# Linear attention with a feed-forward block on one core: softmax reciprocals of k moved to ScalarE, layernorm applies of the k loop moved to VectorE, the Gelu table loaded ahead

## The chip, the cores and the metric

The kernel runs on one core of a Trainium2 chip. The metric is the device time of one execution in microseconds (us), lower being better. One execution of each kernel was profiled. In the profile, PE is TensorE, PEld its weight loads, DVE VectorE, ACT ScalarE and POOL GpSimd; L298 is a line of that kernel's own file, so the same statement has another number in another kernel. All timed runs named here were of the fast state, and comparisons are among those; the one exception, a single look whose state is unknown, is marked.

## The reference, cut to what matters

```python
x = A_x                                            # 1 x 2048 x 640
h = x + A(layernorm(x))                            # linear attention, 32 heads of 20
h2 = h + B(layernorm(h))                           # (gelu(y @ w_gate) * (y @ w_up)) @ w_down

# in A, for each head: q, k, v from x @ wqkv
pq, pk = q @ w_phi, k @ w_phi
phi_q = concat(softmax(pq), softmax(-pq))          # over the 20 features of a head
phi_k = concat(softmax(pk), softmax(-pk))
kv = phi_k^T @ v;  z = sum of phi_k over the sequence
o = (phi_q @ kv) / (phi_q @ z + 1e-6)
```

The sequence is worked in 16 tiles of 128 rows. The softmax of k is not divided out: the kernel keeps E = exp(+-pk), sums it per head (`sk`), and scales v by the reciprocal of the sum (`rs`) instead, once for +pk and once for -pk. So there are two products of v with `rs` per tile, 128x672 elements each.

## The kernel before

The parts that the change touches. `todo` matters: VectorE's product of tile t-1 is put off, and issued between the sum and the reciprocal of tile t.

```python
    def k_tile(t):                       # TensorE: pk; ScalarE: E = exp(+-pk)
        ...
    def k_norm(t):
        sk = small(p1, [P, 2 * H], "sk")
        nc.vector.reduce_sum(sk, Ek[t].rearrange("p s (h f) -> p (s h) f", f=Dh), axis=AX.X)
        if t - 1 in todo:
            todo.pop(t - 1)()
        rs = small(p1, [P, 2 * H], "rs")
        nc.vector.reciprocal(rs, sk)
        Vt[t] = vt = ev.tile([P, 2, H, VC], BF16, name="vt", bufs=8)

        def mult(s, eng):
            eng.tensor_tensor(vt[:, s], vS[t % 6], rs[:, s * H:(s + 1) * H, None].to_broadcast([P, H, VC]), ALU.mult)

        mult(1, nc.gpsimd)
        if t in VP:                      # VP = (0, 2, 4, 6, 9, 11): both products on GpSimd
            mult(0, nc.gpsimd)
        elif t == NT - 1:
            mult(0, nc.vector)
        else:
            todo[t] = lambda: mult(0, nc.vector)
    ...
    for t in range(NT):                  # the k loop, NT = 16
        k_tile(t)
        if t in FQ:                      # FQ = (4, 5, 6, 7, 8): one block of Wq2 a tile,
            fold(WqT, Wq2, True, ...)    # its cast on ScalarE or VectorE by turns
        for j in range(len(QT)):         # QT = (15, 15, 15, 15): after tile 15 the first
            if t == QT[j]:               # four groups of q and their Exp
                q_mm(j)
                q_exp(j)
        if t + 4 < NT:
            v_tile(t + 4)                # TensorE: pv; ScalarE: vS
        if t > 0 and t + 6 < NT:
            ln_ap(t + 6, on_act=True)    # layernorm apply on ScalarE, transposed by DMA
        if t % 2 == 0 and t + 8 < NT:
            ln_st(t + 8, t + 9)          # VectorE: statistics
        k_norm(t)
        if t % 2 == 1 and t >= 5:
            kv_tile(t - 5)               # TensorE: kvp += E^T @ vt
            kv_tile(t - 4)
    ...
    for t in range(12, NT):
        kv_tile(t)
    kv_mask()
    ...                                  # groups q+4.. of q, attention of tiles 0 and 1
    weave(gus(0, 0, 256) + downs(0, (0, 1)), ... attn_at(3, 1, SHORT) ...)
    weave(gus(0, 256, 512) + downs(0, (2, 3)), attn_at(7, 1, SHORT2))
    for b in range(1, NB): ...           # blocks 1 to 3
```

Three words of it: `fold` multiplies one 128-row block of the q weights by w_phi on TensorE (tile `wa`), and a cast on ScalarE or VectorE brings it to `Wq`. `weave` issues a list of TensorE groups, called units here (`gus` are gate and up, `downs` the down projection), and `attn_at(tile, unit, offsets)` says at which unit each of the eight attention stages of a tile goes in between.

The softmax here doesn't subtract the row's maximum and nothing guards it: scores larger than these inputs give would overflow.

Of the kernel before, what the change touches and what calls it, by code (L numbers as in the profile page):

```python
# [8 lines left out]
BF16 = mybir.dt.bfloat16  # L9
F32 = mybir.dt.float32  # L10
ALU = mybir.AluOpType
ACTF = mybir.ActivationFunctionType
AX = mybir.AxisListType
# [4 lines left out]
def kernel(  # L18
# [12 lines left out]
    nc = tc.nc  # L31
    P = 128
    S = 2048
    D = 640
    H = 32
    Dh = 20
    FF = 1536
    NT = S // P
# [9 lines left out]
    VP = (0, 2, 4, 6, 9, 11)  # L48
# [6 lines left out]
    VC = Dh + 1  # L55
# [30 lines left out]
    nhalf = const.tile([P, 2], F32, name="nhalf")  # L86
# [6 lines left out]
    def small(pool, shape, name, bufs=3):  # L93
        return pool.tile(shape, F32, name=name, bufs=bufs)

    def gtile(name):
        return psG.tile([P, 2, 512], F32, name=name, tag="G")

    def ln_stats(pool, tiles, tag, act=True, between=None):

        n = len(tiles)
        mv = small(pool, [P, n, nc.vector.BN_AGGR_DIM], "mv" + tag)
        stats = small(pool, [P, n, 2, nc.vector.BN_STATS_DIM], "stats" + tag)
        for j, xt in enumerate(tiles):
            for i in range(2):
                nc.vector.bn_stats(stats[:, j, i, :], xt[:, i * HD:(i + 1) * HD])  # L106
                if between and i == j == 0:
                    between()
        for j in range(n):
            nc.vector.bn_aggr(mv[:, j, :], stats[:, j])  # L110
        ve = small(pool, [P, n], "ve" + tag)
        nc.gpsimd.tensor_scalar_add(ve, mv[:, :, 1], EPS)
        rstd = small(pool, [P, n], "rstd" + tag)
        nc.gpsimd.tensor_tensor(rstd, ve, nhalf[:, 0:n], op=ALU.pow)  # L114

        mr = small(pool, [P, n], "mr" + tag)
        if act:
            for j in range(n):
                nc.gpsimd.tensor_scalar(mr[:, j:j + 1], mv[:, j, 0:1], rstd[:, j:j + 1], -1.0,
                                        op0=ALU.mult, op1=ALU.mult)  # L120
        return [(xt, mv[:, j, 0:1], rstd[:, j:j + 1], mr[:, j:j + 1]) for j, xt in enumerate(tiles)]
# [26 lines left out]
    p1 = p1_cm.__enter__()  # L148
# [1 line left out]
    Wk2 = p1.tile([P, NC, D], BF16, name="Wk2")  # L150
    acc = p1.tile([P, NC, 4, VC], F32, name="acc")

    vS = [p1.tile([P, H, VC], BF16, name=f"vS{i}") for i in range(6)]
    fp_cm = tc.tile_pool(name="fp", bufs=1, side="right", reuse_waits="tile")
    fp = fp_cm.__enter__()
    WkT = fp.tile([P, NC, D], BF16, name="WkT")
# [7 lines left out]
    for c0, c1 in ((0, 2), (2, 4), (4, 5)):  # L164
        nc.sync.dma_start(Wv[:, c0:c1, :], w_v[:, c0:c1, 2 * D:3 * D])

    ones = fp.tile([P, 2], F32, name="ones")
    nc.scalar.activation(ones, nhalf, ACTF.Exp)
    nc.scalar.dma_start(wphi, phi_v.rearrange("(c p) f -> p c f", p=P))
    nc.sync.dma_start(x_sb[1][:, 0:2, :], x_v[:, 4:6, :])  # L170
    nc.scalar.dma_start(x_sb[1][:, 2:4, :], x_v[:, 6:8, :])
# [8 lines left out]

    zero = fp.tile([P, 512], BF16, name="zero")
    nc.vector.memset(zero, 0.0)
    for i in range(6):
        nc.vector.memset(vS[i][:, :, Dh], 1.0)
    make_identity(nc, ident)
    nc.gpsimd.memset(hmask, 1.0)
# [41 lines left out]
    lnp, Ek, Vt = {}, {}, {}  # L228

    def ln_st(*tiles, act=True, between=None):  # L230
        for t, v in zip(tiles, ln_stats(p1, [x_sb[t // 4][:, t % 4, :] for t in tiles], "1", act, between)):
            lnp[t] = v

    def ln_ap(t, on_act=False, on_pe=False):
        ln = (ln_act if on_act else ln_dve)(p1, "1", *lnp[t])
        if on_pe:
            lnp[t] = ln
        else:
            transpose_to(LN1T[t // 4][:, :, t % 4 * P:(t % 4 + 1) * P], ln, False)
# [28 lines left out]
                                 start=(c == 0), stop=(c == NC - 1))  # L268

    def v_ev(t):  # L270
        nc.scalar.copy(vS[t % 6][:, :, 0:Dh].rearrange("p (u h) f -> p u h f", u=2),
                       pv[t][:, :, 0:HD].rearrange("p u (h f) -> p u h f", f=Dh))

    def v_tile(t):
        v_mm(t)
        v_ev(t)

    def k_tile(t):
        pk = gtile("pk")
        proj(pk, t, Wk2)  # L280
        Ek[t] = ev.tile([P, 2, D], BF16, name="E", bufs=8)
        for s in range(2):
            nc.scalar.activation(Ek[t][:, s, :].rearrange("p (u f) -> p u f", u=2), pk[:, :, 0:HD],  # L283
                                 ACTF.Exp, scale=(1.0 if s == 0 else -1.0))

    def k_norm(t):


        sk = small(p1, [P, 2 * H], "sk")
        nc.vector.reduce_sum(sk, Ek[t].rearrange("p s (h f) -> p (s h) f", f=Dh), axis=AX.X)  # L290
        if t - 1 in todo:
            todo.pop(t - 1)()
        rs = small(p1, [P, 2 * H], "rs")
        nc.vector.reciprocal(rs, sk)  # L294
        Vt[t] = vt = ev.tile([P, 2, H, VC], BF16, name="vt", bufs=8)

        def mult(s, eng):
            eng.tensor_tensor(vt[:, s], vS[t % 6], rs[:, s * H:(s + 1) * H, None].to_broadcast([P, H, VC]), ALU.mult)  # L298

        mult(1, nc.gpsimd)  # L300
        if t in VP:
            mult(0, nc.gpsimd)
        elif t == NT - 1:
            mult(0, nc.vector)
        else:
            todo[t] = lambda: mult(0, nc.vector)

    todo = {}

    def kv_tile(t):  # L310

# [29 lines left out]
    def q_exp(j, signs=(0, 1)):  # L341
        for s in signs:
            nc.scalar.activation(Eq[j][:, :, s, :], pqs[j][:, 0:len(QG[j])], ACTF.Exp, scale=(1.0, -1.0)[s])  # L343
# [21 lines left out]
    v_ev(1)  # L365
    v_tile(2)
    ln_st(4, 5, act=False)
    ln_st(6)
    v_mm(3, (0,))
    fold(WkT, Wk2, False, (0, 1))  # L370
    ln_ap(4, on_pe=True)
# [2 lines left out]
    ln_ap(5, on_pe=True)  # L374
    fold(WkT, Wk2, False, (2, 3, 4))
    ln_tp(4, True)
    ln_st(7)
    fp_cm.__exit__(None, None, None)
    ev_cm = tc.tile_pool(name="ev", bufs=1, side="right", reuse_waits="tile")
    ev = ev_cm.__enter__()  # L380
# [1 line left out]
    for t in range(NT):  # L382
        if t == T3:
            ps_cm.close()
            psG = ps_cm.enter_context(tc.tile_pool(name="psG", bufs=3, space=PSUM, reuse_waits="tile"))
            psK = ps_cm.enter_context(tc.tile_pool(name="psK", bufs=1, space=PSUM, reuse_waits="tile"))
            kvp = psK.tile([P, 2, 512], F32, name="kvp")
        k_tile(t)
        if t == 0:
            ln_tp(5)  # L390
            ln_ap(6)
        if t in FQ:
            fold(WqT, Wq2, True, [i for i, f in enumerate(FQ) if f == t])
        for j in range(len(QT)):
            if t == QT[j]:
                q_mm(j)
                q_exp(j)
        if t + 4 < NT:
            v_tile(t + 4)
        if t > 0 and t + 6 < NT:  # L400
            ln_ap(t + 6, on_act=True)
        if t % 2 == 0 and t + 8 < NT:
            ln_st(t + 8, t + 9)
        k_norm(t)
        if t % 2 == 1 and t >= 5:
            kv_tile(t - 5)
            kv_tile(t - 4)
        if t == 9:
            nc.gpsimd.memset(KV, 0.0)
            nc.gpsimd.memset(kmask, 1.0)  # L410
            for r in HALF:
                nc.gpsimd.affine_select(out=kmask[r], in_=kmask[r], pattern=[[4, NC], [-Dh, 4]],
                                        compare_op=ALU.is_ge, fill=0.0, base=0, channel_multiplier=1)
                nc.gpsimd.affine_select(out=kmask[r], in_=kmask[r], pattern=[[-4, NC], [Dh, 4]],
                                        compare_op=ALU.is_ge, fill=0.0, base=Dh - 1, channel_multiplier=-1)
            nc.gpsimd.tensor_copy(KV[:, :, 0, :, KC - 1], kmask)
            nc.gpsimd.tensor_copy(KV[:, :, 1, :, 0], kmask)
        if t == 10:
            nc.sync.dma_start(Wg, wg_v)
            nc.sync.dma_start(Wo, wo_v)  # L420
            nc.sync.dma_start(Wu, wu_v)
# [10 lines left out]
    p2 = ctx.enter_context(tc.tile_pool(name="p2", bufs=1, reuse_waits="tile"))  # L432
# [107 lines left out]
    def attn_ln(t, on_pe=False):  # L540
        st[t] = (ln_dve if on_pe else ln_act)(p2, "2", *st[t])
# [49 lines left out]
    def weave(units, stages):  # L591

        stages = sorted(later + stages, key=lambda x: x[0])
        later.clear()
        for i, (fn, *args) in enumerate(units):
            while stages and stages[0][0] <= i:
                _, g, *a = stages.pop(0)
                g(*a)
            store(1)
            fn(*args)  # L600
        later.extend((i - len(units), g, *a) for i, g, *a in stages)

    def gus(b, a0, a1):
        return [(gate_up, b, f, a0, a1) for f in range(NF)]

    def downs(b, tls):
        return [(down, b, tl, u) for tl in tls for u in range(2)]
# [30 lines left out]
    attn_e(0, True, True)  # L638
    q_mm(q + 6)
    q_exp(q + 6)  # L640
    attn_ln(1, True)
    attn_e(1, True, True)
    attn_a(2, 2)
# [2 lines left out]
    def attn_at(t, i, offs):  # L646

        fns = (attn_a, attn_b, attn_b2, attn_b3, attn_c, attn_d, attn_d2, attn_e)
        return [(i + o, fn, t) for fn, o in zip(fns, offs) if o >= 0]

    SHORT = (0, 2, 3, 4, 9, 9, 10, 12)
    SHORT2 = (0, 2, 3, 4, 10, 10, 11, 13)
# [3 lines left out]
    weave(gus(0, 0, 256) + downs(0, (0, 1)),  # L656
          attn_at(2, 0, (-1, 0, 1, 2, 7, 7, 8, 10)) + attn_at(3, 1, SHORT) + attn_at(4, 6, SHORT2) + attn_at(5, 9, SHORT2) +
          attn_at(6, 13, SHORT2))
    weave(gus(0, 256, 512) + downs(0, (2, 3)), attn_at(7, 1, SHORT2))
    for b in range(1, NB):  # L660
        stages = []
        if b + 1 < NB:
# [34 lines left out]
```

## Time and profile before

| | before |
|---|---|
| time, median of the runs beside the changed kernel | 281.83 us (281.5 to 282.31) |
| span of the profiled execution | 279.4 us |
| TensorE starts pk of tile 0 | 16.86 us |
| starts the first group of q: end of the k loop | 62.36 us |
| starts the fifth group of q: end of the loop's tail | 72.42 us |
| starts the third gate group: Gelu under way | 95.77 us |
| starts the gate groups of block 1 | 144.07 us |

The marks are start times of TensorE matmuls in the timeline. Since TensorE hardly waits between them, the distance of two marks is the time of that part of the program: 45.50 us for the loop, 10.06 for its tail, 23.35 from there to the third gate group, 48.30 from there to block 1. I use the same marks for every kernel below.

The profile's groups of instructions, one shape each, say what the parts cost. The columns are line, engine, operation, output and inputs, shapes, count, then busy us and mean ns of one, then the idle time of the engine ahead of them:

```profile
L298 POOL TENSOR_TENSOR vt<-vS,rs 128x672 bf16<-128x672 bf16 x22 | 29.2, 1345 | 9.1 <-DVE rs L294 8.5 <-ACT E L283 0.4
L290 DVE TENSOR_REDUCE sk<-E 128x64 f32<-128x1280 bf16 x16 | 23.3, 1455 | 3.4 <-ACT E L283 3.4
L298 DVE TENSOR_TENSOR vt<-vS,rs 128x672 bf16<-128x672 bf16 x10 | 8.8, 882 | 0.1
L130 DVE TENSOR_SCALAR ln<-x_sb,mv,rstd 128x640 bf16<-128x640 bf16 x9 | 3.9, 443 | 2.4 <-POOL rstd L114 2.4
```

A product costs 1.35 us on GpSimd and 0.88 on VectorE, a layernorm apply on VectorE 0.44. Now see in the timeline of tile 5 (start, duration, engine, operation) when the two engines multiply:

```profile
34.24 0.85 DVE L298 TENSOR_TENSOR vt<-vS,rs 128x672 bf16<-128x672 bf16 x1
...
35.01 0.55 DVE L294 RECIPROCAL rs<-sk 128x64 f32<-128x64 f32 x1
...
35.64 4.03 POOL L298 TENSOR_TENSOR vt<-vS,rs 128x672 bf16<-128x672 bf16 x3 [0.18 <-DVE rs L294]
```

VectorE's product is over before its reciprocal releases GpSimd. The order of the program keeps the two apart in six of VectorE's ten products (0.85 us each) and lets VectorE begin first in the last (0.86, at 69.12); three near the loop's end begin in the last 0.2 to 0.3 us of a product of GpSimd and take 0.93 to 1.01. I did not see what that was worth when I predicted.

### The profile page before, as it was taken

The numbers are of one execution on the slowest core, as the hardware profiler recorded it, in microseconds if no ns is written. First come the engines' busy times: TensorE is split into PE (matmuls) and PEld (weight loads), VectorE is DVE, ScalarE is ACT, GpSimd is POOL, SyncE is SP. The second block draws the span as 40 slices with busy tenths as digits, with TensorE's granted clock in tenths as the row PEclk, the third lists the DMA queues.
The fourth block names the chain that finished last, engine by engine and source line by source line (L and its number), as shares of the span: only waits on it lengthen the run. The fifth ranks groups of instructions, "written<-read, shape, count | busy, mean of one in ns | idle before, by whom it ended". The sixth has DMA issues, their size and how long they took to land.

```text
span 279.4 us, 5750 instructions
## 1 busy us (share of the span) xinstructions
PE 271.9 (97%) x2326; PEld 171.5 (61%) x2326; DVE 166.0 (59%) x289; ACT 139.9 (50%) x226; POOL 96.5 (35%) x211
## 2 busy tenths in 40 slices
PE   5899999999999999999999999999999999999995
PEld 2676677774655788788764555675455567444573
DVE  5899998789396586676324848322667532333222
ACT  2589888758596847355434454413446340222200
POOL 5448986794302216453401243300135230000000
PEclk9999999999999999999999999999999999999999
DMA  7991323694440021322520103221031513000011
GB/s 231 265 260 25 55 49 46 176 396 158 142 145 0 2 45 29 70 50 68 52 70 2 36 20 66 42 77 47 2 47 23 74 23 94 26 1 0 0 49 47
DMA packets 40347, 21.05 MB, mean 75 GB/s; under 512 B 33152, under 2 KB 38400, under 8 KB 40320
## 3 DMA queue, kind: packets, MB, share of 16 engines
q1 hardware_dynamic: 39376, 20.16, 28.8%
q10 hardware_dynamic: 944, 0.52, 0.7%
q8 instruction: 18, 0.29, 0.5%
q14 instruction: 9, 0.07, 0.1%
HBM read 10.18 MB, written 2.62 MB: 46 GB/s over the span
## 4 chain that ended last, share of the span: by engine, by line
PE 89%; DVE 4%; ACT 3%; DMA 1%; POOL 1%; issue 1%; ACTq 0%
PE gu L554 37%; PE pd L569 19%; PE pq L338 8%; PE po L509 8%; PE pk L251 7%; PE pv L251 5%; PE ab L449 2%; PE kvp L316 2%; DVE stats L106 1%; DMA x_sb<-in_A_x_dram 1%; DVE sk L290 1%; ACT E L283 1%; POOL rstd L114 1%; ACT Eq L343 1%; PE wa L215 1%
## 5 line engine op out<-in xcount | busy, mean ns | idle before, releaser
L557 ACT ACTIVATE g<-gu 128x512 bf16<-128x512 f32 (+1 forms) x60 | 30.7, 512 | 76.1 <-PE gu L554 75.1
L560 DVE TENSOR_TENSOR GT<-gu,g 128x512 bf16<-128x512 f32 (+1 forms) x60 | 34.5, 581 | 53.6 <-ACT g L557 53.4
L554 PE MATMUL gu<-LN2T,Wg 128*128 128x512 bf16 (+1 forms) x300 | 61.9, 337 | 0.5 <-DVE GT L560 0.4
L554 PE MATMUL gu<-LN2T,Wu 128*128 128x512 bf16 (+1 forms) x300 | 61.7, 336 | 0.0
L569 PE MATMUL pd<-Wd,GT 128*128 128x320 bf16 x384 | 53.8, 299 | 0.0
L569 PEld LDWEIGHTS <-GT 128*128 128x128 bf16 x384 | 37.4, 98 | 15.7 <-DVE GT L560 0.9
L554 PEld LDWEIGHTS <-Wu 128*128 128x128 bf16 x300 | 29.4, 98 | 22.6
L554 PEld LDWEIGHTS <-Wg 128*128 128x128 bf16 x300 | 28.4, 98 | 21.3 <-issue 0.5
L251 PEld LDWEIGHTS <-LN1T 128*128 128x128 bf16 x300 | 28.5, 98 | 11.6 <-issue 0.7
L298 POOL TENSOR_TENSOR vt<-vS,rs 128x672 bf16<-128x672 bf16 x22 | 29.2, 1345 | 9.1 <-DVE rs L294 8.5
L575 DVE TENSOR_TENSOR y<-pd,x_sb 128x640 bf16<-128x640 f32 (+1 forms) x17 | 13.3, 784 | 30.6 <-PE pd L569 30.6
L457 ACT COPY AB<-ab 128x704 f32<-128x704 f32 x28 | 19.5, 748 | 13.7 <-PE ab L449 13.5
L290 DVE TENSOR_REDUCE sk<-E 128x64 f32<-128x1280 bf16 x16 | 23.3, 1455 | 3.4 <-ACT E L283 3.4
L490 DVE TENSOR_TENSOR tt<-AB,w 128x1280 bf16<-128x1280 f32 x16 | 23.8, 1486 | 2.1 <-POOL w L483 2.0
L251 PE MATMUL pk<-Wk,LN1T 128*128 128x320 bf16 x160 | 24.1, 299 | 0.4 <-ACT E L283 0.3
L509 PE MATMUL po<-Wo,oT 128*128 128x320 bf16 x160 | 24.4, 299 | 0.0
L283 ACT ACTIVATE E<-pk 128x640 bf16<-128x640 f32 x32 | 20.8, 705 | 6.9 <-PE pk L251 6.7
L338 PE MATMUL pq<-LN1T,Wq 128*128 128x512 bf16 x100 | 22.9, 379 | 0.0
L251 PE MATMUL pv<-Wv,LN1T 128*128 128x320 bf16 x140 | 21.3, 299 | 0.0
L343 ACT ACTIVATE Eq<-pq 128x1024 bf16<-128x1024 f32 (+1 forms) x22 | 19.4, 950 | 3.7 <-PE pq L338 3.7
L509 PEld LDWEIGHTS <-oT 128*128 128x128 bf16 x160 | 15.6, 98 | 7.2 <-ACT oT L139 0.2
L125 ACT ACTIVATE ln<-x_sb,v,rstd 128x640 bf16<-128x640 bf16 x14 | 12.9, 919 | 10.5 <-POOL v L537 10.3
(80 smaller groups left out, 258.8 us busy)
## 6 DMA issues: line engine op xcount, KB each, us to landing
out_dram<-y SPq DMA_DIRECT2D x15, 160.0 KB, 1.8
Wg<-in_B_w_gate_dram SPq DMA_DIRECT2D x1, 1920.0 KB, 7.6
Wu<-in_B_w_up_dram SPq DMA_DIRECT2D x1, 1920.0 KB, 15.1
Wd<-in_B_w_down_dram SPq DMA_DIRECT2D x1, 1920.0 KB, 8.0
x_sb<-in_A_x_dram SPq DMA_DIRECT2D x2, 640.0 KB, 4.7
Wo<-in_A_wo_dram SPq DMA_DIRECT2D x1, 800.0 KB, 9.3
x_sb<-in_A_x_dram SPq DMA_DIRECT2D x2, 320.0 KB, 4.8
Wv<-in_A_wqkv_dram SPq DMA_DIRECT2D x2, 320.0 KB, 6.2
```

The costliest lines, as they stand in the source:

```text
L251: nc.tensor.matmul(ps[:, u, 0:HD], lhsT=lnT(t, c), rhs=W[:, c, u * HD:(u + 1) * HD], start=(c == 0), stop=(c == NC - 1))
L283: nc.scalar.activation(Ek[t][:, s, :].rearrange("p (u f) -> p u f", u=2), pk[:, :, 0:HD], ACTF.Exp, scale=(1.0 if s == 0 else -1.0))
L290: nc.vector.reduce_sum(sk, Ek[t].rearrange("p s (h f) -> p (s h) f", f=Dh), axis=AX.X)
L298: eng.tensor_tensor(vt[:, s], vS[t % 6], rs[:, s * H:(s + 1) * H, None].to_broadcast([P, H, VC]), ALU.mult)
L338: nc.tensor.matmul(pqs[j][:, i, :], lhsT=Wq2[:, kc, c * P:(c + 1) * P], rhs=LN1T[b][:, kc, :], start=(kc == 0), stop=(kc == NC - 1))
L343: nc.scalar.activation(Eq[j][:, :, s, :], pqs[j][:, 0:len(QG[j])], ACTF.Exp, scale=(1.0, -1.0)[s])
L490: nc.vector.tensor_tensor(tt.rearrange("p s (h f) -> p s h f", f=Dh), num, w[:, :, :, None].to_broadcast([P, 2, H, Dh]), ALU.mult)
L509: nc.tensor.matmul(po[:, u, 0:HD], lhsT=st[t][:, c, :], rhs=Wo[:, c, u * HD:(u + 1) * HD], start=(c == 0), stop=(c == NC - 1))
L554: nc.tensor.matmul(gu[:, i, 0:n], lhsT=W[:, c, f * P:(f + 1) * P], rhs=LN2T[b][:, c, a0:a1], start=(c == 0), stop=(c == NC - 1))
L557: nc.scalar.activation(g[:, 0:n], gu[:, 0, 0:n], ACTF.Gelu_apprx_tanh)
L560: nc.vector.tensor_tensor(st[b, "g", f][:, a0:a1], gu[:, 1, 0:n], g[:, 0:n], ALU.mult)
L569: nc.tensor.matmul(pd[:, u, 0:HD], lhsT=st[b, "g", f][:, tl * P:(tl + 1) * P], rhs=Wd[:, f, u * HD:(u + 1) * HD], start=(f == 0), stop=(f ...
```

## The change

The intent: take the slow reciprocal (547 ns a tile) off VectorE by computing 1/S as exp(-ln S) on ScalarE, where Ln and Exp can live in one table set; in exchange move the loop's layernorm applies from ScalarE, where one costs 933 ns, to VectorE, where it costs 443; and load the Gelu table ahead of the first Gelu by a dummy. With `rs` no longer made on VectorE, its products are issued plainly, one tile later, after the sum. A seventh `vS` buffer makes room for the delay, and the attention of tile 7 moves two units later in its weave.

```diff
-    vS = [... for i in range(6)]
+    vS = [... for i in range(7)]                       # and every t % 6 becomes t % 7
-    nc.scalar.activation(ones, nhalf, ACTF.Exp)
+    nc.scalar.add_instruction(mybir.InstLoadActFuncSet(..., act_func_set_id=6))
@@ k_tile, after the two Exp of tile t
+        if t > 0:
+            k_rs(t - 1)
+    def k_rs(t):
+        sk = st1[t]
+        nc.scalar.activation(sk, sk, ACTF.Ln)
+        st1[t] = rs = small(p1, [P, 2 * H], "rs")
+        nc.scalar.activation(rs, sk, ACTF.Exp, scale=-1.0)
@@ k_norm
-        nc.vector.reduce_sum(sk, Ek[t]..., axis=AX.X)
-        if t - 1 in todo:
-            todo.pop(t - 1)()
-        nc.vector.reciprocal(rs, sk)
+        for s in range(2):
+            nc.vector.reduce_sum(sk[:, s * H:(s + 1) * H], Ek[t][:, s, :]..., axis=AX.X)
+    def k_vt(t):
+        for s in (1, 0):
+            eng = nc.gpsimd if s == 1 or t in VP else nc.vector
+            eng.tensor_tensor(vt[:, s], vS[t % 7], rs[...].to_broadcast(...), ALU.mult)
@@ the loop
-            ln_ap(t + 6, on_act=True)
+            ln_ap(t + 6)
-            ln_st(t + 8, t + 9)
+            ln_st(t + 8, t + 9, act=False)           # ln_st(6), ln_st(7) ahead of the loop too
         k_norm(t)
+        if t > 0:
+            k_vt(t - 1)
+        if t == NT - 1:
+            k_rs(t)
+            k_vt(t)
@@ after the last Exp of q
+    nc.scalar.activation(dummy, nhalf, ACTF.Gelu_apprx_tanh)
@@ the second weave
-    ... attn_at(7, 1, SHORT2))
+    ... attn_at(7, 3, SHORT2))
```

More of the change, by code (lines that the diff above doesn't have):

```diff
@@ L151 @@
     acc = p1.tile([P, NC, 4, VC], F32, name="acc")
-    vS = [p1.tile([P, H, VC], BF16, name=f"vS{i}") for i in range(6)]
+    vS = [p1.tile([P, H, VC], BF16, name=f"vS{i}") for i in range(7)]
     fp_cm = tc.tile_pool(name="fp", bufs=1, side="right", reuse_waits="tile")
@@ L165 @@
         nc.sync.dma_start(Wv[:, c0:c1, :], w_v[:, c0:c1, 2 * D:3 * D])
-    ones = fp.tile([P, 2], F32, name="ones")
-    nc.scalar.activation(ones, nhalf, ACTF.Exp)
+    nc.scalar.add_instruction(mybir.InstLoadActFuncSet(name=nc.get_next_instruction_name(), act_func_set_id=6))
     nc.scalar.dma_start(wphi, phi_v.rearrange("(c p) f -> p c f", p=P))
@@ L182 @@
     nc.vector.memset(zero, 0.0)
-    for i in range(6):
+    for i in range(7):
         nc.vector.memset(vS[i][:, :, Dh], 1.0)
@@ L270, in v_ev @@
     def v_ev(t):
-        nc.scalar.copy(vS[t % 6][:, :, 0:Dh].rearrange("p (u h) f -> p u h f", u=2),
+        nc.scalar.copy(vS[t % 7][:, :, 0:Dh].rearrange("p (u h) f -> p u h f", u=2),
                        pv[t][:, :, 0:HD].rearrange("p u (h f) -> p u h f", f=Dh))
@@ L284, in k_tile @@
                                  ACTF.Exp, scale=(1.0 if s == 0 else -1.0))
-    def k_norm(t):
-        sk = small(p1, [P, 2 * H], "sk")
-        nc.vector.reduce_sum(sk, Ek[t].rearrange("p s (h f) -> p (s h) f", f=Dh), axis=AX.X)
-        if t - 1 in todo:
-            todo.pop(t - 1)()
-        rs = small(p1, [P, 2 * H], "rs")
-        nc.vector.reciprocal(rs, sk)
-        Vt[t] = vt = ev.tile([P, 2, H, VC], BF16, name="vt", bufs=8)
-        def mult(s, eng):
-            eng.tensor_tensor(vt[:, s], vS[t % 6], rs[:, s * H:(s + 1) * H, None].to_broadcast([P, H, VC]), ALU.mult)
-        mult(1, nc.gpsimd)
-        if t in VP:
-            mult(0, nc.gpsimd)
-        elif t == NT - 1:
-            mult(0, nc.vector)
-        else:
-            todo[t] = lambda: mult(0, nc.vector)
-    todo = {}
+        if t > 0:
[5 more added lines that the diff above has]
+        nc.scalar.activation(rs, sk, ACTF.Exp, scale=-1.0)
+    st1 = {}
+    def k_norm(t):
+        st1[t] = sk = small(p1, [P, 2 * H], "sk")
+        for s in range(2):
+            nc.vector.reduce_sum(sk[:, s * H:(s + 1) * H], Ek[t][:, s, :].rearrange("p (h f) -> p h f", f=Dh), axis=AX.X)
+    def k_vt(t):
+        rs = st1[t]
+        Vt[t] = vt = ev.tile([P, 2, H, VC], BF16, name="vt", bufs=8)
+        for s in (1, 0):
+            eng = nc.gpsimd if s == 1 or t in VP else nc.vector
+            eng.tensor_tensor(vt[:, s], vS[t % 7], rs[:, s * H:(s + 1) * H, None].to_broadcast([P, H, VC]), ALU.mult)
     def kv_tile(t):
@@ L367 @@
     ln_st(4, 5, act=False)
-    ln_st(6)
+    ln_st(6, act=False)
     v_mm(3, (0,))
@@ L376 @@
     ln_tp(4, True)
-    ln_st(7)
+    ln_st(7, act=False)
     fp_cm.__exit__(None, None, None)
@@ L640 @@
     q_exp(q + 6)
+    dummy = small(p2, [P, 2], "dummy", 1)
+    nc.scalar.activation(dummy, nhalf, ACTF.Gelu_apprx_tanh)
     attn_ln(1, True)
@@ L658 @@
           attn_at(6, 13, SHORT2))
-    weave(gus(0, 256, 512) + downs(0, (2, 3)), attn_at(7, 1, SHORT2))
+    weave(gus(0, 256, 512) + downs(0, (2, 3)), attn_at(7, 3, SHORT2))
     for b in range(1, NB):
```

## The prediction

> **What bounds the kernel now.** I read the page's first two parts, then TensorE's waits, the chain in order of time, and the timeline at the four places that the diff touches: the k loop, its end, the first Gelu, the hand-over to block 1.
>
> ```profile
> PE 271.9 (97%) x2326; PEld 171.5 (61%) x2326; DVE 166.0 (59%) x289; ACT 139.9 (50%) x226; POOL 96.5 (35%) x211
> PEclk9999999999999999999999999999999999999999
> ...
> PE gu L554 <- DVE GT L560: 0.4, 1, 0.4
> PE pk L251 <- ACT E L283: 0.3, 1, 0.3
> ```
>
> TensorE is busy for 97% of the span at full clock. A busy TensorE need not be at its peak, so I checked the chain's pieces: ten matmuls of 320 columns take 1.36 us there, ten of 512 take 2.17, in every stage alike, which is 0.42 ns a column throughout. From 16.86 us to 276.5 the chain is such pieces, apart from a stretch near 21 to 31 us (where TensorE is busy beside it) and one near 91.6 to 95.8. So there is next to nothing to take out of the middle: TensorE's waits after the start-up are 0.3 us for a buffer of pk, 0.4 for one of gu, and some tenths between pieces. The 59% of VectorE is an average: by stretches it is busy 14.36 of the 14.74 us from 16.86 on and 13.88 of the next 14.40. In the k loop it is the second bound.
>
> The loop's end, from the timeline:
>
> ```profile
> 69.03 2.92 ACT L343 ACTIVATE Eq<-pq 128x1024 bf16<-128x1024 f32 x4 [0.22 <-PE pq L338]
> 69.12 0.86 DVE L298 TENSOR_TENSOR vt<-vS,rs 128x672 bf16<-128x672 bf16 x1
> 69.19 1.97 POOL L298 TENSOR_TENSOR vt<-vS,rs 128x672 bf16<-128x672 bf16 x1 [1.34 <-DVE rs L294]
> 70.00 2.36 PEld L316 LDWEIGHTS <-E 128*64 128x64 bf16 x120 [0.42 <-issue]
> 70.00 2.49 PE L316 MATMUL kvp<-vt,E 128*64 128x84 bf16 x120
> ```
>
> The scaled v of the last tile, 15, is made at 69.1 to 71.2 us, while ScalarE works on the four Eq pairs until 71.95; TensorE multiplies tiles 10 to 15 from 70.0 and tile 15 comes last, from about 72.1. It just fits.
>
> The first Gelu:
>
> ```profile
> 91.62 1.94 ACT L343 ACTIVATE Eq<-pq 128x1024 bf16<-128x1024 f32 x2 [0.50 <-PE pq L338]
> 93.58 1.28 ACT L557 ACT_TABLE_LOAD   x1
> 94.88 0.38 ACT L557 ACTIVATE g<-gu 128x256 bf16<-128x256 f32 x1
> 95.29 0.42 DVE L560 TENSOR_TENSOR GT<-gu,g 128x256 bf16<-128x256 f32 x1 [1.20 <-ACT g L557]
> 95.77 0.71 PE L554 MATMUL gu<-LN2T,Wg 128*128 128x256 bf16 x5 [0.37 <-DVE GT L560]
> ```
>
> The load already starts 0.02 us after the last Exp ends; it waits for nothing else. The hand-over of tile 7 to block 1:
>
> ```profile
> 136.09 0.81 DVE L523 SCALAR_TENSOR_TENSOR x_sb<-po,x_sb 128x640 bf16<-128x640 f32 x1
> ...
> 139.75 0.92 ACT L125 ACTIVATE ln<-x_sb,v,rstd 128x640 bf16<-128x640 bf16 x1 [1.49 <-POOL v L537]
> ...
> 144.07 1.25 PE L554 MATMUL gu<-LN2T,Wg 128*128 128x512 bf16 x5
> ...
> LN2T<-ln SPq DMA_TRANSPOSE x14, 2.6
> ```
>
> The layernorm ends at 140.67, the transposing DMA lands 2.6 later, 143.3, and the matmul that needs it starts at 144.07: some 0.8 us of slack.
>
> **What the Trainium skill says.** "ScalarE: Activation LUTs", section "Table sets: the hidden batching unit": one set holds ln and exp, so both need one load. The diff loads a set by number, which I take to be that one; the trace before shows one load at the start and one before Gelu, Copy, Identity and Square running in both; I expect two again. Its section "What ACT_TABLE_LOAD costs" gives an ACTIVATE with immediates 186 ns + 0.833 ns an element: 239 ns for 64, an estimate; the trace agrees roughly (128x2 took 203 ns, 128x512 took 597; the load 1283, as the page has it). "Perfetto Trace Analysis", section "Tensor Engine Instruction (MATMUL, LD_WEIGHTS)", says that ScalarE, VectorE and GpSimd are strict FIFO; the trace agrees, everything in program order. "GPSIMD Engine Reference", section "Specifications", names contention for SBUF with VectorE instructions of two SBUF inputs: a product on GpSimd takes 1.32 us, but 1.97 where VectorE's product of 0.86 starts beside it.
>
> **The change part by part.**
>
> 1. Reciprocals. VectorE loses 16 x 547 ns = 8.8 us. ScalarE gets Ln and Exp per tile: 2 x 239 plus a hand-over, about 0.5 us (estimate), 8 us in all. The sum over h is split: VectorE's products of 256 and 512 elements take 416 and 690 ns, so some 142 ns of an instruction are fixed; I pay them once more a tile, +0.13 where the two overlap a little (estimate), 2 us in all.
>
> 2. Layernorm applies, 9 of them. ScalarE loses 9 x 933 = 8.4 us, VectorE gains 9 x 0.44 = 4.0. GpSimd loses the small products of L119. Sums: ScalarE about -0.4, VectorE -8.8+2+4.0 = -2.8, but nearly all of that after tile 9; while the applies run, VectorE changes by -0.46+0.13+0.40 = +0.07 us a tile (from a start to the next: reciprocal 65.82 to 66.28, apply 9.35 to 9.75).
>
> 3. In the loop TensorE runs without a gap, so less work elsewhere gives at most the 0.3 of the pk wait plus about 0.1. Against it: ScalarE now waits for VectorE. Exp of tile t is followed by Ln of tile t-1, which needs the sum of t-1. Before, the sum of tile 4 ended at 34.33 and Exp of tile 5 at 34.74, that of tile 6 at 41.39 and Exp of 7 at 41.74: 0.4 us of slack. Going through tiles 4 to 9 by hand with these durations, ScalarE, now earlier, waits 0.5 us at each such sum, TensorE gains 0.4 at tile 5 and gives it back in the v buffers at tiles 6 to 9. I put the loop at 0 (-0.4 to +0.8). The seventh vS buffer takes away ScalarE's 1.5 us of waits (vS for vt), inside the same account.
>
> 4. The loop's end. In program order Ln and Exp of tile 15 now stand on ScalarE after the four Eq pairs, which follow TensorE and end at 71.95. So its reciprocals come at 71.95+0.5 = 72.45 instead of 69.0. Then the two products start together: VectorE 0.86, to 73.35; GpSimd 1.97, to about 74.45. TensorE ends tile 14 near 72.1 and waits; ten matmuls of tile 15 follow GpSimd's product, 0.22. The stage ends at 74.7 instead of 72.49: **+2.2 us** (+1.5 if GpSimd takes 1.32). What follows (mask, copy, products: 1.77 us before) still lies behind q's ten matmuls of 2.27.
>
> 5. Gelu's load. It was early already. The dummy ACTIVATE after it takes about 0.2 (203 ns for 128x2) ahead of the first real Gelu, whose product releases the gu buffer TensorE waits for: **+0.15**.
>
> 6. attn 7 two units later. Its last stage then has offset 16 in a weave of 16 units and slips to the head of the next, before block 1's first gate matmul, which needs it. Its po moves from ahead of unit 11 to ahead of unit 13, so after po TensorE has three half downs (6.52 us for four, 1.63 each) and one ab (0.50): 5.39 us. The chain after po, from tile 6, whose Square waits for no Gelu: VectorE starts 131.34, Square 132.20, layernorm 134.53 to 135.45, issue, 2.6 to landing: 138.07, that is 6.73, plus 0.06 from po's end, 6.8. TensorE waits 6.8-5.39 = **+1.4**.
>
> Sum: 0+2.2+0.15+1.4 = 3.75; I take 0.25 off because po, Gelu or GpSimd's product may sit a little better than drawn: +3.5, 281.9+3.5 = **285.4 us**.
>
> **The rivals.** (a) The intended gain: ScalarE and VectorE relieved, TensorE faster. For it: ScalarE's waits for vt, the pk wait. Against: all TensorE waits outside the start-up that these could free sum to under 1 us, so at best 281.0. (b) ScalarE takes VectorE's place and the cross wait breaks the loop: if each of some eight tiles lost 0.5 us more, +4, then 289. For: VectorE 97% busy there. Against: the order of VectorE's work stays the same and its time per tile grows by only 0.07. (c) The loop's end costs nothing: if the products of tile 15 were ready by 72.1, the sum falls to about +1.5, 283.4. Against: ScalarE's order. (d) Sets switch at each Ln: 32 loads of 1.28 us, 41 us; I give it 1%, since one set serves both.
>
> **Range and chances.** The additions at 4 and 6 are independent: losing either gives 283 to 284, the loop going badly adds up to 1, a slowed clock after the pause up to 1.5 (the start-up has a pause of 1.7 us without one). The range is **283.2 to 287.3**. Two per cent are 5.6 us: slower by that needs rival (b), **0.07**; faster needs 5.6 us that TensorE doesn't have, **0.01**; same **0.92**.
>
> **What would show it.** Right: a TensorE wait of about 2 us before kvp's last matmuls, put down to vt on GpSimd; a second of about 1.4 before gu of block 1, released by the DMA into LN2T; the gu wait for GT at 0.5 instead of 0.4; ScalarE waiting for sk in the loop; two table loads. If kvp shows no wait, step 4 is wrong; if gu of block 1 doesn't wait for LN2T, step 6 is; if pv waits for vS by several tenths per tile, step 3 was too kind. A span below 281 would mean that TensorE's pieces themselves became shorter, which nothing here foresees.

## The result, and the profile after

The changed kernel takes 289.59 us (median of 4, 288.89 to 291.28) against 281.83 for the kernel before: the ratio is 1.0283, with a 95% interval of 1.0236 to 1.0329. It is slower by over 2%, and the time lies outside the predicted range. Such a ratio is the mean time of one kernel's fast runs over that of the other's fast runs of the same rounds, so it is not quite the ratio of the medians quoted. The slowest of the four, 291.28, had a mean granted clock of 0.988; the other three lie within 0.75 us.

| part | before | after | difference | predicted |
|---|---|---|---|---|
| start, to pk of tile 0 | 16.86 | 17.43 | +0.57 | 0 |
| k loop, to the first group of q | 45.50 | 49.39 | **+3.89** | 0 (-0.4 to +0.8) |
| tail, to the fifth group of q | 10.06 | 12.51 | +2.45 | +2.2 |
| to the third gate group | 23.35 | 23.44 | +0.09 | +0.15 |
| to block 1 | 48.30 | 49.77 | +1.47 | +1.4 |
| the rest of the span (279.4 and 287.9) | 135.3 | 135.4 | 0 | 0 |

The start is nothing of the change's: over the kernels below, which have the same program up to there but for small things, that mark lies anywhere from 16.49 to 17.69. What is left is the loop. TensorE's waits in the changed kernel (what waited, what ended the wait, us in total, times, longest) show by which doors it came in:

```profile
PE pk L250 <- DVE Wq L225: 2.8, 2, 1.8
PE gu L560 <- DMA LN2T<-ln: 1.4, 1, 1.4
PE kvp L317 <- DVE vt L308: 1.3, 1, 1.3
...
PE wa L214 <- ACT Wq L223: 1.1, 1, 1.1
PE kvp L317 <- POOL vt L308: 0.8, 1, 0.8
...
PE gu L560 <- DVE GT L566: 0.5, 1, 0.5
```

The two waits of kvp are the tail (step 4), the one of gu for LN2T is the hand-over (step 6), and gu for GT is 0.5 where it was 0.4 (step 5): all three as foreseen. New are 2.8 us in which pk waits for VectorE's casts of Wq, and 1.1 us in which the fold waits for ScalarE's. Together they are 3.9 us, the size of the loop's loss. ScalarE's cast comes late because ScalarE stood waiting for VectorE's sum just before it (1.64 us, until 33.12). VectorE's casts and sums come late because its own work has grown:

```profile
L308 POOL TENSOR_TENSOR vt<-vS,rs 128x672 bf16<-128x672 bf16 x22 | 32.5, 1500 | 12.9 <-ACT rs L292 12.8
L300 DVE TENSOR_REDUCE sk<-E 128x32 f32<-128x640 bf16 x32 | 24.4, 804 | 2.5 <-ACT E L282 2.4
L308 DVE TENSOR_TENSOR vt<-vS,rs 128x672 bf16<-128x672 bf16 x10 | 14.7, 1468 | 4.5 <-ACT rs L292 4.5
L130 DVE TENSOR_SCALAR ln<-x_sb,mv,rstd 128x640 bf16<-128x640 bf16 x18 | 9.8, 550 | 2.5 <-POOL rstd L114 2.5
```

The same product of the same size takes VectorE 1468 ns where it took 882: 5.9 us more in ten. The nine layernorm applies of the loop cost 9.8-3.9 = 5.9 us, 0.66 each, where 0.44 were put down. The split sums cost 1.1 us more, not 2. So VectorE, which loses 8.8 us of reciprocals, ends up with 5.9+5.9+1.1-8.8 = 4.1 us more over the whole kernel, where the prediction had it 2.8 us lighter. The timeline of the changed kernel shows what lies beside the long ones:

```profile
28.25 4.56 POOL L308 TENSOR_TENSOR vt<-vS,rs 128x672 bf16<-128x672 bf16 x3
28.49 1.79 DVE L308 TENSOR_TENSOR vt<-vS,rs 128x672 bf16<-128x672 bf16 x1
...
30.20 1.43 DVE L130 TENSOR_SCALAR ln<-x_sb,mv,rstd 128x640 bf16<-128x640 bf16 x1
...
36.33 4.55 POOL L308 TENSOR_TENSOR vt<-vS,rs 128x672 bf16<-128x672 bf16 x3
...
36.59 1.77 DVE L308 TENSOR_TENSOR vt<-vS,rs 128x672 bf16<-128x672 bf16 x1
...
38.28 0.81 DVE L225 CAST Wq<-wa 128x640 bf16<-128x640 f32 x1
...
39.14 1.52 PE L250 MATMUL pk<-Wk,LN1T 128*128 128x320 bf16 x10 [1.84 <-DVE Wq L225]
```

`rs` has been ready since 26.48 and 33.67, and GpSimd starts its products as soon as its own small layernorm work is done, at 28.25 and 36.33, while VectorE is still in the sum; VectorE's product and its apply then run beside them and come out 0.9 and 1.0 us too long. Behind the second such product stands the cast, and behind the cast TensorE, idle for 1.84 us. The tail shows the reverse order of starts:

```profile
76.64 0.26 ACT L292 ACTIVATE rs<-sk 128x64 f32<-128x64 f32 x1
76.93 0.86 DVE L308 TENSOR_TENSOR vt<-vS,rs 128x672 bf16<-128x672 bf16 x1 [4.49 <-ACT rs L292]
76.97 1.99 POOL L308 TENSOR_TENSOR vt<-vS,rs 128x672 bf16<-128x672 bf16 x1 [5.58 <-ACT rs L292]
77.84 0.38 PE L317 MATMUL kvp<-vt,E 128*64 128x84 bf16 x10 [1.27 <-DVE vt L308]
79.01 0.38 PE L317 MATMUL kvp<-vt,E 128*64 128x84 bf16 x10 [0.79 <-POOL vt L308]
```

Here VectorE was idle and began 0.04 us ahead; it took its 0.86, and GpSimd paid with 1.99. As predicted, the products of tile 15 come only after Ln and Exp, which stand behind the four Exp pairs of q.

### The profile page after: what moved, and what is told of

Same layout as the page of the kernel before. It is cut to its first block, busy times and chain, and to the rows that moved or that the text cites. A ratio compares the mean times of both kernels' runs of the same rounds, so it can differ in the third digit from the quotient of the medians.

```text
span 287.9 us, 5757 instructions
## 1 busy us (share of the span) xinstructions
PE 274.6 (95%) x2326; PEld 173.1 (60%) x2326; DVE 170.3 (59%) x299; ACT 138.5 (48%) x249; POOL 95.9 (33%) x201
## 4 chain that ended last, share of the span: by engine, by line
PE 83%; DVE 7%; ACT 4%; DMA 2%; issue 2%; POOL 1%; POOLq 0%; ACTq 0%
PE gu L560 36%; PE pd L575 17%; PE po L515 8%; PE pq L339 7%; PE pk L250 5%; PE pv L250 4%; DVE sk L300 2%; PE ab L455 2%; ACT Eq L344 2%; DVE stats L106 2%; PE pv L266 1%; PE kvp L317 1%; DMA x_sb<-in_A_x_dram 1%; PE tp L138 1%; DVE ln L130 1%
## 5 line engine op out<-in xcount | busy, mean ns | idle before, releaser
L308 POOL TENSOR_TENSOR vt<-vS,rs 128x672 bf16<-128x672 bf16 x22 | 32.5, 1500 | 12.9 <-ACT rs L292 12.8
L300 DVE TENSOR_REDUCE sk<-E 128x32 f32<-128x640 bf16 x32 | 24.4, 804 | 2.5 <-ACT E L282 2.4
```

What stands on the lines that cost most here:

```text
L300: nc.vector.reduce_sum(sk[:, s * H:(s + 1) * H], Ek[t][:, s, :].rearrange("p (h f) -> p h f", f=Dh), axis=AX.X)
L308: eng.tensor_tensor(vt[:, s], vS[t % 7], rs[:, s * H:(s + 1) * H, None].to_broadcast([P, H, VC]), ALU.mult)
```

## The experiments

**Theory.** VectorE's products and applies collide with GpSimd's products over access to SBUF. The Trainium skill says this on a page that the prediction did not use: "SBUF — State Buffer", section "Who interferes with whom", lets a VectorE instruction with two SBUF inputs, or one in a 2-port mode (which a tensor_scalar can enter), contend with GpSimd (the former where GpSimd's instruction reads SBUF, as its products do), and holds that whoever issues first gets the shared pair for the whole instruction while the other blocks. The old order mostly kept them apart, the new one does not.
**Rival 1.** ScalarE now waits in order for VectorE's sums, which breaks the loop (rival (b) of the prediction). **Rival 2.** VectorE has simply more work: split sums and applies. **Rival 3.** The loss is in the tail and the later parts, and the loop only shifts.

All by the marks of the timeline, in us; ratios against the kernel before in the same rounds.

| kernel | loop | tail | ratio (95%) |
|---|---|---|---|
| before | 45.50 | 10.06 | 1 |
| after | 49.39 | 12.51 | 1.0283 (1.0236 to 1.0329) |
| e1_tails | 49.40 | 10.07 | 1.0131 (1.0116 to 1.0146) |
| e2_apart | 47.03 | 12.52 | 1.0211 (1.0185 to 1.0238) |
| e3_ln_on_act | 46.88 | 12.52 | 1.0196 (1.0163 to 1.0229) |
| e4_rs_lag2 | 47.49 | 14.58 | 1.0351 (1.0331 to 1.0371) |
| e5_ln_dve_alone | 48.07 | 10.16 | 1.0101 (1.0075 to 1.0126) |
| e6_before_side | 46.67 | 10.16 | 1.0033 (1.0022 to 1.0044) |
| e7_pool_tiny | 45.05 | 11.53 | 1.0094 (1.0067 to 1.0120) |
| e8_small | 45.90 | 10.06 | 1.0048 (1.0029 to 1.0067) |
| e9_order_only | 46.55 | 10.07 | 1.0029 (1.0020 to 1.0038) |
| e10_order_apart | 46.86 | 10.06 | 1.0040 (1.0026 to 1.0053) |
| e12_gelu_gap | 45.48 | 10.07 | 0.9986 (0.9974 to 0.9998) |

Each mark is from one profile. Kernels with the same loop agree to 0.02 us (before and e12, the changed kernel and e1) or to 0.33 (e3 and e9, which differ only at tile 15), so I read nothing into differences of the loop under some 0.4 us.

**e1_tails: undo the three later parts, keep the loop.** From the changed kernel:

```diff
+        if t == NT - 1: k_norm(t)              # ahead of the q groups
         ... q_mm(j); q_exp(j)
+                if j == 1: k_rs(t)             # Ln, Exp of tile 15 after two Exp pairs, not four
-    nc.scalar.activation(dummy, nhalf, ACTF.Gelu_apprx_tanh)
-    attn_at(7, 3, SHORT2)
+    attn_at(7, 1, SHORT2)
```

> The changed kernel with three of its parts undone: tile 15's Ln and Exp moved ahead of the last two Eq pairs, attn 7 back at offset 1, no dummy Gelu. The k loop is left as changed. If the working of steps 4, 5 and 6 holds: from the first pq to the fifth pq 12.4 falls to about 10.0 us, from the first to the second block of gates 49.8 falls to 48.3, the wait for GT falls by 0.1, and the time to about 285.6 (4 us less than the changed kernel). Rival: the stalls only move, e.g. to the next stage, and the time stays above 287.5. The k loop stays at 49.5 us under every theory.

The median is 284.76 us. The tail falls back to 10.07, the wait for GT to 0.4, the way to block 1 to 48.30; the loop stays at 49.40. Steps 4, 5 and 6 are right in place and size, and rival 3 falls: the loop's 3.9 us are a loss by themselves.

**e2_apart: four of VectorE's products away from GpSimd's.** From the changed kernel, the products of tiles 1, 3, 5 and 7 are issued three tiles later, after the statistics, with eight vS buffers:

```diff
+            if eng is nc.vector and t in LATE:        # LATE = (1, 3, 5, 7)
+                late[t] = vt, rs
+                continue
...
+        if t - 3 in late:
+            k_late(t - 3)
         k_norm(t)
```

> The changed kernel with VectorE's products of tiles 1, 3, 5 and 7 issued three tiles later, after the statistics, where GpSimd has no product; same instructions, same work. Theory side by side (VectorE's and GpSimd's products now start together and slow each other): these four products fall from about 1.75 us to 0.85, and the k loop (first pk to first pq) from 49.6 to 47 us or less, the time by 2.5 or more. Theory more work (VectorE simply has too much) and theory cross wait (ScalarE's Ln waits for VectorE's sums in order): loop within 0.5 us of 49.6.

The loop falls by 2.4 us to 47.03, and the four moved products take 825 ns. Yet not all comes back: now the applies find GpSimd at work and take its time in turn.

```profile
31.16 1.25 DVE L130 TENSOR_SCALAR ln<-x_sb,mv,rstd 128x640 bf16<-128x640 bf16 x1
```

Besides an eighth vS buffer, for which ScalarE had not waited in the changed kernel, only the place of four products changed, so 2.4 us of the loop's loss hang on what they met. The collision was moved as much as removed; the applies of the whole kernel go from 550 to 652 ns on the mean.

**e3_ln_on_act: the layernorm applies back on ScalarE.** From the changed kernel:

```diff
-            ln_ap(t + 6)
+            ln_ap(t + 6, on_act=True)
-            ln_st(t + 8, t + 9, act=False)
+            ln_st(t + 8, t + 9)                       # and ln_st(6), ln_st(7)
```

> The changed kernel with the loop's layernorm applies back on ScalarE; reciprocals stay on ScalarE. Theory more work: the loop returns to 45.7 us, as VectorE is again no busier than before. Theory side by side: VectorE's products stay at 1.5 us or more, but VectorE has some 5 us less (0.66 a tile instead of 0.44, those beside GpSimd), so the loop comes to 46 to 47.5. Theory cross wait: ScalarE has the waits and the applies, loop at 49 or longer.

The loop is 46.88, 2.5 us better. The products still take 1350 ns on the mean (the expectation said 1.5 us or more), so the applies are not the whole of it. Two of the four runs, the profiled one among them, had a mean clock of 0.994 and were some 1.8 us longer than the other two, so the ratio of 1.0196 overstates what the loop alone would make of it.

**e4_rs_lag2: ScalarE's Ln and Exp one tile later still, so that it never waits for a sum.**

```diff
-        if t > 0: k_rs(t - 1)
+        if t > 1: k_rs(t - 2)
-        if t > 0: k_vt(t - 1)
+        if t > 1: k_vt(t - 2)                         # and tiles 14, 15 at the end
```

> The changed kernel with Ln, Exp and the products one tile later, so that ScalarE never waits for a sum that is still being made. Theory cross wait: the loop falls from 49.6 to 46 us or less. Theory side by side: the products still start together, loop within 1 us of 49.6 and VectorE's products still at 1.5 us in the mean. Theory more work: no change.

The loop is 47.49, 1.9 us better, and ScalarE's waits for sums are gone, but VectorE's products still take 1487 ns. Both theories missed the loop: the cross wait asked for 46 or less, side by side for 48.6 or more. TensorE no longer waits for Wq or for the fold at all; what it waits for instead, 1.7 us in pv, is ScalarE's copy to vS, as ScalarE now waits 6.3 us for vS buffers that the later products hold. The experiment thus opened a new wait, and 1.9 us is no measure of what the cross wait passes on: it may be more. Rival 1 has a part, as a door: VectorE's lateness reached TensorE as it did because ScalarE waits in order. It isn't where the lateness comes from, as e7 below shows. As a whole the kernel is worse, since two tiles' products now stand at the end (tail 14.58), and around the waits there the clock dropped: it is 0.63 of full speed between 75 and 80 us.

**e5_ln_dve_alone: from the kernel before, only the applies moved to VectorE.**

```diff
-            ln_ap(t + 6, on_act=True)
+            ln_ap(t + 6)
-            ln_st(t + 8, t + 9)
+            ln_st(t + 8, t + 9, act=False)            # and ln_st(6), ln_st(7)
```

> The kernel before with one part alone: the nine layernorm applies of the loop on VectorE, reciprocals still on VectorE. VectorE was busy 41.7 of the loop's 45.5 us and gets 4 to 6 more. Theory side by side: its products stay at 0.85 to 1.0 us, as the reciprocal between them keeps them apart; the applies beside GpSimd's products go above 0.44; loop 46.5 to 48.5. Theory more work: 48 to 50, as this puts more on VectorE than the whole change does. Theory cross wait: 45.5, as ScalarE doesn't wait for VectorE's sums here.

The loop takes 48.07, 2.6 us more, with the reciprocals and the sums untouched and no Ln on ScalarE. The loop's applies take 0.58 us on the mean; TensorE waits 1.9 us for the transposed layernorm, which comes later. The cross wait is ruled out here, but 48.07 lies in the ranges of both other theories: VectorE gets 9 x 0.44 = 4.0 us of plain work and 1.3 of collision, and this run does not tell them apart.

**e6_before_side: from the kernel before, VectorE's product not put off.** It comes right after the reciprocal that also releases GpSimd:

```diff
-            todo[t] = lambda: mult(0, nc.vector)
+            mult(0, nc.vector)
```

> The kernel before with one line of order changed: VectorE's product follows its reciprocal at once instead of the next tile's sum, so it starts together with GpSimd's. Theory side by side: VectorE's products rise from 0.88 us to 1.5 or more, and the loop from 45.5 to 47.5 or more. Theories more work and cross wait: nothing is added and ScalarE waits for no sum, so products 0.88 and loop within 0.5 us of 45.5.

This is a miss in its first number and instructive for it. The products do run side by side, but VectorE's take 946 ns on the mean, not 1.5 us; GpSimd's rise from 1345 to 1578. The loop is 1.2 us longer, not 2, with a new TensorE wait of 1.2 for the transposed layernorm. I took each product with its start from the trace: in seven of VectorE's ten it starts 0.04 to 0.14 us ahead of GpSimd's, takes 0.86, and GpSimd's takes 1.90 to 1.99. VectorE needs no signal to go on from its own reciprocal; GpSimd does. So who starts first keeps its time, as the skill's page says. Doing the same count for the changed kernel, eight of VectorE's ten products start inside a running product of GpSimd, and each ends 0.70 to 0.72 us after that one ends, whatever their own start was: the one at 28.49 waits for GpSimd's, which ended at 29.57, and ends at 30.28. Four applies that start so end 0.18 to 0.19 us after it. And a product of GpSimd that comes up in the meantime takes 1.93 us beside a product and 1.40 beside an apply, instead of 1.32.

**e7_pool_tiny: from the changed kernel, GpSimd's products cut to two of 32 heads.** They keep their place and their release; the matmul takes a constant tile in place of their output. The result is wrong on purpose.

```diff
-            eng.tensor_tensor(vt[:, s], vS[t % 7], rs[...], ALU.mult)
+            if s == 1 or t in VP:                    # sc: a small tile that nobody reads
+                nc.gpsimd.tensor_tensor(sc, vS[t % 7][:, 0:2, :], rs[:, s * H:s * H + 2, None]..., ALU.mult)
+                src[t, s] = vfix                       # a constant
+            else: ...                                # VectorE's product as before, src[t, s] = vt
```

> The changed kernel with GpSimd's products of the loop cut to two of 32 heads, the matmuls reading a constant tile in their place (the result is wrong on purpose). VectorE's and ScalarE's instructions, their order and ScalarE's waits for sums stay as changed. Theory side by side: VectorE's products go to 0.85 us, the applies to 0.44, and the loop from 49.4 to 46.3 or less. Theories more work and cross wait: the loop stays above 48.5. The stall at the loop's end shrinks to VectorE's product (12.5 to about 11.5) under each.

The loop falls from 49.39 to 45.05 us, below the kernel before. All of VectorE's work, its order, and ScalarE's cross wait are still there:

```profile
L314 DVE TENSOR_TENSOR vt<-vS,rs 128x672 bf16<-128x672 bf16 x10 | 8.5, 850 | 5.9 <-ACT rs L294 5.9
L130 DVE TENSOR_SCALAR ln<-x_sb,mv,rstd 128x640 bf16<-128x640 bf16 x18 | 7.9, 441 | 2.5 <-POOL rstd L114 2.5
L311 POOL TENSOR_TENSOR sc<-vS,rs 128x42 f32<-128x42 bf16 x22 | 6.0, 286 | 29.9 <-ACT rs L294 29.9
```

The products are at 850 ns, the applies at 441, ScalarE's waits for a sum are gone from its list, and TensorE waits neither for Wq nor for the fold. One could object that the constant also frees TensorE from waiting for GpSimd; but in the changed kernel it never waited for GpSimd within the loop, only once in the tail. Nor does VectorE gain by a wait: in both kernels the only thing it waits for in the loop is Exp's E (2.4 us in the changed kernel, 4.7 here). Rivals 1 and 2 fall as causes: without GpSimd's load beside it, the changed loop takes 45.05 us, no longer than the old one's 45.50.

**e8_small: from the kernel before, two small parts.** A seventh vS buffer and the attention of tile 3 one unit later, to get Gelu's first product out of its way:

```diff
+    vS = [... for i in range(7)]                      # and every t % 6 becomes t % 7
-    attn_at(3, 1, SHORT)
+    attn_at(3, 2, SHORT)
```

> The kernel before with two small things: seven instead of six buffers for v, and attn 3 one unit later, so that the third gate group takes a free buffer instead of waiting for the first Gelu behind the table load. If TensorE's own waits are what is left to gain: the wait for Exp of E at tile 5 (0.3 us) and the pauses near the first Gelu (some 0.7 us) go, 0.5 to 1.1 us less, ratio 0.996 to 0.998. Rival: the waits move to the next buffer and the ratio stays within 0.001 of 1.

A miss: 282.95 us. The wait for GT stays at 0.4, and the later tile 3 now makes gu wait 1.4 us for the DMA into LN2T.

**e9_order_only and e10_order_apart: what is left when all else is undone.** The first is the changed kernel with e1's three undone and the applies back on ScalarE; only the reciprocals on ScalarE, the split sums and the seventh buffer remain. The second moves four products as e2 did.

```diff
# e9: e1_tails and e3_ln_on_act together;   e10: e9 and
+        if t - 3 in late:
+            k_late(t - 3)
```

> The changed kernel with the three tails undone and the layernorm applies back on ScalarE: of the change only the reciprocals on ScalarE, the split sums and the seventh buffer are left. If the costs add (loop 46.9 us as with the applies back alone, the rest as before): 1.4 us over the kernel before, ratio 1.005, about 283. Rival: with the applies back ScalarE's two extra instructions a tile still cost more, ratio 1.01 or above.

> The same, and VectorE's products of tiles 1, 3, 5, 7 issued three tiles later, after the statistics. Theory side by side: what is left of the loop's loss goes, loop 45.3 to 46.2 us, ratio 0.999 to 1.003, and no faster than before by more than 0.2%, as TensorE has no more waits to give. Rival: reciprocals on ScalarE do pay once nothing collides, ratio below 0.997.

Moving the reciprocals alone gives 282.23 us and a loop 1.05 longer than before; the products take 1258 ns, and TensorE's new waits in the loop are 1.2 us for the transposed layernorm. The applies alone cost 2.6 (e5). For e10 the expectation of 45.3 to 46.2 missed: 46.86, no better. By their starts, three of the four moved products again began inside one of GpSimd's, and the four took 1196 ns. What fills that time now and did not in e2 I did not settle. Moving an instruction three tiles does not by itself keep it apart; in the kernel before an order did, since the reciprocal that releases GpSimd follows VectorE's product.

**e11_probe: the disputed cost by itself.** From the kernel before, with both engines multiplying, applying and summing side by side after the kernel's own work. Its time and its state (one look) don't matter, only durations within it:

```diff
+    for k in range(3):
+        for _ in range(4): prod(nc.gpsimd, pc, pb)
+        for _ in range(6):
+            if k == 0:   prod(nc.vector, pb2, pa)
+            elif k == 1: nc.vector.tensor_scalar(pl, xt, ..., op0=ALU.subtract, op1=ALU.mult)
+            else:        nc.vector.reduce_sum(ps2, ..., axis=AX.X)
```

> The kernel before with a probe after its end, the collision measured by itself: VectorE's product of 672 elements alone; six of them beside four of GpSimd's; six applies of 640 elements beside four; six sums of 640 beside four; GpSimd's product alone. Theory side by side: VectorE's product above 1.1 us beside GpSimd against 0.85 alone, the apply above 0.6 against 0.44, the sum unchanged at 0.80, and GpSimd's product longer beside the first two only. Rival (what lengthened them in the loop was something else, e.g. the DMA or ScalarE): all at their lone durations.

The view of one tile gives shortest, median and longest duration in ns; the last line is the page's group of the sums (128x32 here, half a tile's):

```profile
L674 POOL TENSOR_TENSOR pc<-pb,pr x15: 1315/1316/1859, 283.3 to 309.7; 128x672 bf16<-128x672 bf16 x15
L674 DVE TENSOR_TENSOR pb<-x_sb,pr x11: 851/859/1856, 278.8 to 291.6; 128x672 bf16<-128x672 bf16 x11
L684 DVE TENSOR_SCALAR pb<-x_sb,pr x6: 440/1337/1357, 293.1 to 299.2; 128x640 bf16<-128x640 bf16 x6
```

```profile
L686 DVE TENSOR_REDUCE ps<-x_sb 128x32 f32<-128x640 bf16 x6 | 4.9, 818 | 0.2
```

The shortest are those alone, the longest those beside the other engine: VectorE's product 0.85 and 1.86, GpSimd's 1.32 and 1.86, the apply 0.44 and 1.36. The sums, of one input, stay at 818 against 807 alone. One part missed: beside the applies GpSimd's product was expected to be longer, and only the first of four was (1.45), while the other three, which had each begun before the apply that met them, took 1.32. That is the theory without the kernel around it.

**e12_gelu_gap: another try at Gelu's first wait.** From the kernel before, tile 3's attention starts two units later with its stages closer together, so that its copies don't stand ahead of the first Gelu products while its last stage stays at the same unit, 13:

```diff
-    attn_at(3, 1, SHORT)
+    attn_at(3, 3, (0, 1, 2, 3, 7, 7, 8, 10))
```

> The kernel before with attn 3's first stage two units later (after the third gate group), its last four stages at the units where they were. The third gate group then needs no buffer that the first Gelu frees, and the hand-over of tile 3 keeps its time. If TensorE's pause there is what can still be gained: no wait for GT, 0.4 to 0.6 us less, ratio 0.998. Rival: the wait moves on to the next buffer, ratio 1.000 or above.

The wait for GT is gone from TensorE's list, and block 1 starts at 143.50 instead of 144.07. The median is 281.03 us of 22 runs: 0.14% faster than the kernel before in the same rounds (281.46), with an interval that just stays below 1, and the second of two tries: a small gain at most. It is the one use I found for what the change wanted at Gelu: not an earlier table, but less in front of the first product.

## Why the prediction was wrong, and where it was right

**The step that failed** is the pair of steps 2 and 3: "VectorE changes by +0.07 us a tile", and from it "I put the loop at 0 (-0.4 to +0.8)". The loop lost 3.89 us. The instruction counts were right; what failed is that each duration was taken from the kernel before, where the order of the program mostly kept VectorE's products away from GpSimd's. In the changed kernel the products cost 1.47 instead of 0.88 and the loop's applies 0.66 instead of 0.44. e7_pool_tiny shows that this, and not the work or the waits as such, is the cause: take GpSimd's load away and the loop is at 45.05. e11_probe shows the same of single instructions. The wait that the prediction did put on ScalarE, in order for VectorE's sum, then helped to carry the lateness to TensorE (e4).

It could have been seen. The prediction quoted GpSimd's 1.97 beside VectorE's 0.86, cited the contention for SBUF, and used it, correctly, for the one place where it drew the two products side by side, the tail. In the loop it did not ask what the removed `todo` line had done. It also had only the half of the rule that it needed: it knew that GpSimd pays where VectorE starts first, not that VectorE pays where GpSimd does.

**Step 1.** ScalarE's Ln and Exp take 258 and 256 ns against 239 estimated; the table is loaded twice as expected. The split sums cost 1.1 us, not 2. Neither moved the result. The prediction counts a reciprocal in two ways, 547 ns in the sum of -2.8 and 0.46 us (from start to start) in the +0.07; by the second the sum is -1.4.

**Step 3's own waits.** ScalarE does wait for sums, though in two waits of 1.6 and 0.7 us and not 0.5 at each tile; but the sign that was to tell, pv waiting for vS, never came; the lateness went through the casts of Wq (2.8) and the fold (1.1) instead.

**Step 4** was right: +2.45 for +2.2, with the waits of kvp where they were drawn (1.27 and 0.79) and GpSimd at 1.99 for 1.97. **Step 5**: +0.09 for +0.15. **Step 6**: +1.47 for +1.4, by the wait of 1.4 named. The 0.25 taken off because something might sit better did not come.

**The rivals.** (a), (c) and (d) fall. (b) named the size of the loop's loss, +4, by luck, as it put it down to the order wait alone: that wait passes lateness on (e4), and costs nothing where VectorE is on time (e7). Its chance of 0.07 rested on the 0.07 us a tile. With the 3.89 in place of 0 the prediction's own sum gives 7.6 instead of 3.75, close to the 7.9 that the four parts of the table add up to.

**What stays open.** That e5's 2.6 and e9's 1.05 add up to 3.6 of 3.9 us is no proof of parts: there TensorE waits for the transposed layernorm, in the changed kernel for the casts, and some of e5's loss may be plain work. How much each collision costs TensorE depends on what stands behind it in its queue, and I did not take that apart further. A version with the reciprocals on ScalarE and an enforced order of the two engines' products was not built.

## What to carry to other kernels

Before a product on VectorE is moved or released by another engine, look in the timeline at what GpSimd does at that moment: where their instructions contend (here products and applies, not sums), the two engines are one resource, and the one that starts second waits for the first to end. An odd deferral in a tuned kernel may be there for that, so ask what a removed line kept apart. And durations read from a profile hold only with the neighbours they had there.

## What the Trainium skill lacked or had wrong

- "SBUF — State Buffer", "Who interferes with whom": right on who contends and that the first to start wins, and on sums not contending (818 ns against 807). "Fully blocks" for the whole instruction is, taken by the durations of the profile, a little too strong: in the probe alternating products of the two started every 1.89 us, where 0.86 + 1.32 are 2.18, and a blocked VectorE product ended 0.70 to 0.72 us after GpSimd's, an apply 0.18, less than their 0.85 and 0.44 alone. That the fixed part of an instruction overlaps with the wait is a guess.
- "GPSIMD Engine Reference", "Specifications": names the contention without a size and without saying who pays (the SBUF page says who); in the changed kernel and the probe a 128x672 product took 0.84 to 1.86 us on VectorE and 1.31 to 1.99 on GpSimd, a 128x640 apply 0.43 to 1.43.
- "ScalarE: Activation LUTs", "What ACT_TABLE_LOAD costs": its formula gives 239 ns for 64 elements; Ln and Exp of 128x64 took 258 and 256.
- "TensorE: Matmul & The Clock Gate", "🎯 Why this matters for your kernels", warns of gaps over about 3 us. In e3_ln_on_act two waits of 1.28 and 0.79 us, with 0.38 us of matmuls between them, were followed by a mean clock of 0.66 from 75 to 80 us; in the changed kernel's profiled run waits of the same length left it at 1.00. No run here shows what decides it.
